# A convolution on four 64-by-64 tiles, its input staged in blocks of 64 tokens, and the first groups transposed inside PSUM

## The chip, the cores and the metric

The kernel runs on one core of one Trainium2 chip. The metric is device time in microseconds (us) of one execution; the kernel before takes 362.98 us (median of three runs, 361.67 to 363.38). The kernels here are told apart by the ratio of mean times of runs made on the same chip in the same rounds, and by their profiles. "Group" below means eight output tiles of 128 tokens; the program has 33 groups.

## The reference, cut to what matters

```python
# attention part: a causal convolution over time, 7 taps, one set of taps per head
w = softmax(weight)                          # 8 heads x 7 taps
y[b, s, h*24+g] = sum_k w[h, k] * x[b, s-6+k, h*24+g]     # B=8, S=4224, D=192
# mixer part
h = (y^T @ U) @ V                            # rank 32, over the whole sequence
u = y + h^T
out = u + relu(u @ w_ch1) @ w_ch2            # 192 -> 768 -> 192
```

The product `y^T @ U` runs over the whole sequence. So no token of a batch can go through the mixer before the convolution of that whole batch is done. The batches then follow one another.

## The kernel before

The convolution is a matmul with a band matrix as the stationary operand. Batch 0 uses the whole 128x128 array; batches 1 to 7 use sixteen 32x32 tiles, so their input lies in blocks of 32 tokens, a quarter of the sequence in each 32 partitions.

```python
def load_x(b, r, ...):                       # GpSimd's queue: fp32 in DRAM, bf16 in SBUF
    n = 4 * n_of(r, NX)
    nc.gpsimd.dma_start(out=x_bufs[b % 2][32 * r : 32 * r + 32, 1 : 1 + n, :], in_=tokens(b, r, 0, n))
    ...                                      # and the six tokens before the quarter

def conv_unit(b, heads):                     # two heads: 64 matmuls
    ps = [bank() for _ in range(4)]
    for i, h in enumerate(heads):
        for k in range(2):                   # this block, the block before
            for r in range(4):               # rows of the array, one PSUM bank each
                for c in range(4):           # columns of the array
                    nc.tensor.matmul(out=..., lhsT=band_of(r, h, k), rhs=x_bufs[b % 2][rows, ...], ...)
    ...                                      # four evictions by ScalarE

# the head of the program: batch 0
for i, (a, e) in enumerate(CHUNKS):          # four chunks of fp32 input, SyncE's queue
    ...cast by ScalarE and VectorE, conv_first(a, e), U's transposes, keep_warm(3), tt_part
tt_split(0, ...); tt_sum(0, "act")
h_unit(0)
transpose_pe(0)                              # u of group 0 by TensorE through PSUM
h_unit(1)
transpose(1)                                 # u of group 1 by a DMA transpose
```

Each group `g` then runs, on TensorE: perhaps a conv unit of a later batch, W1 (36 matmuls), h of group `g+2` (8 matmuls), W2 of group `g-1` (48 matmuls). VectorE adds `u` to what W2 leaves in PSUM, into one of four output tiles, and SyncE's queue stores it. The same queue carries the DMA transposes of `u`.

## Time and profile before

| reading | us |
|---|---|
| median | 362.98 |
| first W1 starts | 35.5 |
| steady group without / with a conv unit | 8.33 / 9.06 |
| one conv unit | 0.72 |
| longest wait of TensorE | 8.1 |

From the page of the kernel before, the slices of the span: the busy share of TensorE in tenths and the clock granted to it. One digit is a fortieth of the span, 9 us.

```profile
PE   5697999994699999999999999999999999999995
PEclk9587899999599999999999999999999999999999
```

The last three quarters of the span are full. What can be won lies in the first eleven slices, about 100 us: the head, and the hole in slices 10 and 11. The table of stretches says the same in numbers. Its columns are the stretch and its length, then for each engine the busy time (and instructions), then the clock, the DMA share and GB/s.

```profile
core 0: us, PE busy (x) PEld busy (x) DVE busy (x) ACT busy (x) POOL busy (x), PEclk, DMA share, GB/s
0.00:35.50 35.50, 25.08 (x191) 14.35 (x194) 14.86 (x46) 13.07 (x26) 10.67 (x23) 0.76 1.05 187
35.50:84.70 49.20, 47.25 (x895) 30.99 (x894) 37.55 (x70) 29.18 (x61) 9.64 (x20) 0.97 1.22 161
84.70:101.30 16.60, 8.51 (x166) 3.72 (x164) 4.30 (x7) 5.65 (x12) 2.51 (x5) 0.69 0.72 118
101.30:362.60 261.30, 255.66 (x4000) 179.14 (x3998) 207.00 (x385) 131.54 (x260) 20.88 (x42) 1.00 0.73 152
```

The hole, in the timeline of TensorE (start, length, engine, line, operation, what it writes and reads, and in brackets the idle time before it and what ended that):

```profile
85.28 0.50 PE L260 MATMUL bank<-x_sb_86,band 32*32 32x216 bf16 x12
93.87 0.39 PE L260 MATMUL bank<-x_sb_86,band 32*32 32x192 bf16 x16 [8.09 <-DMA x_sb_86<-in_x_dram]
...
94.72 6.70 PE L380 MATMUL bank<-uT,W_sb 64*128 64x512 bf16 x36
```

TensorE starts batch 3's convolution (line 260) and waits 8.09 us for its input. The W1 behind it (line 380) takes 6.70 us where 4.06 is usual, because the clock is at half (0.5 from 89.9 to 100.1 us in the clock record). The steady half, from the chain of waits (start, length, what):

```profile
278.31 0.73 PE bank L260 x55
279.04 3.99 PE bank L380 x36
283.03 0.32 PE bank L331 x8
283.35 4.07 PE bank L401 x48
```

Conv unit, W1, h, W2, and nothing but TensorE between them.

### The profile page before, as it was taken

What the parts mean: (1) busy time and instruction counts of PE and PEld (TensorE: products, weight loads), DVE (VectorE), ACT (ScalarE), POOL (GpSimd) and SP (SyncE); (2) the same over time, 40 slices, a digit from 0 to 9 for tenths busy, and PEclk for the clock granted to TensorE, in tenths of its full rate; (3) what the DMA queues carried; (4) which work ended last, traced back from release to release, by engine and by line L of the source; (5) the groups of instructions that cost most, each with busy time, mean ns of one, the idle gap of its engine ahead of it and who ended that gap; (6) DMA issues with size and microseconds to landing.
All of it is one profiled execution on the core that took longest, in us unless ns stands there. A gap on an engine that the chain in (4) does not pass through costs nothing. (4 is left out here: it accounts for less than half of the span.)

```text
span 362.6 us, 12101 instructions
## 1 busy us (share of the span) xinstructions
PE 336.5 (93%) x5248; PEld 228.2 (63%) x5250; DVE 263.7 (73%) x506; ACT 179.4 (49%) x358; POOL 43.7 (12%) x90
## 2 busy tenths in 40 slices
PE   5697999994699999999999999999999999999995
PEld 2363466654277666666666666667666766667775
DVE  4335767863268887888788878887888888888763
ACT  2344774571345546555655554554455355555440
POOL 2143140131101111111111111110000000000000
PEclk9587899999599999999999999999999999999999
DMA  5989999999557997999999988898444556555525
GB/s 161 253 152 181 104 139 217 157 186 200 60 130 114 148 195 142 175 176 177 181 164 180 181 163 164 169 181 170 118 121 129 106 127 174 152 132 132 132 96 167
DMA packets 122837, 56.23 MB, mean 155 GB/s; under 512 B 84224, under 2 KB 122624, under 8 KB 122624
## 3 DMA queue, kind: packets, MB, share of 16 engines
q1 hardware_dynamic: 90512, 42.60, 49.4%
q0 software_dynamic: 32128, 12.83, 32.3%
q8 instruction: 41, 0.67, 0.7%
q14 instruction: 12, 0.10, 0.1%
q10 hardware_dynamic: 144, 0.03, 0.0%
HBM read 28.93 MB, written 25.95 MB: 151 GB/s over the span
## 5 line engine op out<-in xcount | busy, mean ns | idle before, releaser
L380 PE MATMUL bank<-uT,W_sb 64*128 64x512 bf16 x1188 | 139.0, 385 | 0.1
L65 ACT ACTIVATE y_sb<-bank 128x432 bf16<-128x432 f32 (+5 forms) x122 | 51.0, 505 | 105.6 <-PE bank L260 82.1
L380 PEld LDWEIGHTS <-W_sb 64*128 64x128 bf16 x1188 | 57.7, 96 | 69.6 <-issue 10.8
L411 DVE TENSOR_TENSOR o<-bank,u_ring 128x384 f32<-128x384 f32 x132 | 70.6, 553 | 27.8 <-PE bank L401 24.4
L342 DVE TENSOR_TENSOR u_ring<-y_sb,bank 128x384 bf16<-128x384 bf16 (+1 forms) x136 | 64.3, 535 | 3.7 <-PE bank L331 3.6
L260 PEld LDWEIGHTS <-band 32*32 32x32 bf16 x1568 | 15.5, 88 | 18.1 <-DMA x_sb_86<-in_x_dram 8.3
L99 POOL CAST seen<-y_sb 1x1 f32<-1x1 bf16 x24 | 4.2, 173 | 167.4 <-ACT y_sb L65 167.4
L260 PE MATMUL bank<-x_sb_86,band 32*32 32x192 bf16 (+1 forms) x896 | 14.0, 255 | 9.3 <-DMA x_sb_86<-in_x_dram 8.1
L103 POOL DMA_DIRECT2D x_sb_86<-in_x_dram x16 | 12.9, 806 | 5.0 <-PE bank L380 3.1
L331 PE MATMUL bank<-tt_sb,V_sb 32*128 32x192 bf16 x264 | 13.1, 252 | 0.4 <-ACT tt_sb L65 0.4
L331 PEld LDWEIGHTS <-V_sb 32*128 32x128 bf16 x264 | 5.2, 93 | 12.7 <-issue 12.3
L284 PE MATMUL bank<-x_sb_85,band 128*128 128x288 bf16 (+3 forms) x32 | 8.6, 316 | 4.1 <-ACT x_sb_85 L65 3.9
L310 DVE TENSOR_TENSOR lo<-bank,hi 128x192 bf16<-128x192 f32 x8 | 2.9, 358 | 12.9 <-ACT hi L65 12.9
L67 DVE CAST y_sb<-bank 128x288 bf16<-128x288 f32 (+3 forms) x10 | 4.9, 488 | 8.5 <-PE bank L284 8.4
L260 PE MATMUL bank<-x_sb_85,band 32*32 32x192 bf16 (+1 forms) x672 | 9.5, 251 | 1.4 <-issue 0.8
L103 POOL DMA_DIRECT2D x_sb_85<-in_x_dram x12 | 9.7, 807 | 4.4 <-PE bank L380 2.4
L201 PE MATMUL bank<-warm 128*128 128x512 bf16 x23 | 8.6, 508 | 1.3 <-DVE warm L136 1.2
L391 DVE TENSOR_SCALAR rl_1832<-bank 128x512 bf16<-128x512 f32 x2 | 1.4, 692 | 10.9 <-PE bank L380 10.9
L260 PE MATMUL bank<-x_sb_86,bandp 32*32 32x192 bf16 x128 | 8.6, 250 | 0.0
L284 PE MATMUL bank<-x_sb_85,bandp 128*128 128x288 bf16 (+3 forms) x32 | 8.5, 314 | 0.0
L297 PE MATMUL bank<-y_sb,U_sb 128*32 128x192 bf16 x264 | 7.9, 248 | 0.6 <-DVE y_sb L67 0.5
L284 PEld LDWEIGHTS <-band 128*128 128x128 bf16 x32 | 3.7, 120 | 5.7 <-issue 4.5
(323 smaller groups left out, 631.6 us busy)
## 6 DMA issues: line engine op xcount, KB each, us to landing
out_dram<-o SPq DMA_DIRECT2D x132, 192.0 KB, 3.1
x_sb_86<-in_x_dram POOLq DMA_DIRECT2D x12, 384.0 KB, 6.9
x_sb_85<-in_x_dram POOLq DMA_DIRECT2D x9, 384.0 KB, 7.6
x_sb_86<-in_x_dram POOLq DMA_DIRECT2D x4, 432.0 KB, 7.6
x_sb_85<-in_x_dram POOLq DMA_DIRECT2D x3, 432.0 KB, 5.7
xf<-in_x_dram SPq DMA_DIRECT2D x1, 1152.0 KB, 12.7
xf<-in_x_dram SPq DMA_DIRECT2D x1, 960.0 KB, 15.0
W_sb<-in_moe_w_ch_dram POOLq DMA_DIRECT2D x3, 288.0 KB, 6.9
```

The lines of the kernel that those rows point to most:

```text
L65: nc.scalar.activation(out=out_ap, in_=in_ap, func=ACT.Copy)
L67: nc.vector.tensor_copy(out=out_ap, in_=in_ap)
L99: nc.gpsimd.tensor_copy(out=seen[0:1], in_=y_tiles[b - 1][0:1, 0, seen_col : seen_col + 1])
L103: nc.gpsimd.dma_start(out=x_bufs[b % 2][32 * r : 32 * r + 32, 1 : 1 + n, :], in_=tokens(b, r, 0, n))
L201: nc.tensor.matmul(out=ps[:], lhsT=warm[:, 0:P], rhs=warm[:], start=True, stop=True)
L260: nc.tensor.matmul(out=o.rearrange("p (t g) -> p t g", g=nh * GS)[:, :, i * GS : (i + 1) * GS], lhsT=band_of(r, h, k), rhs=x_bufs[b % 2][r ...
L284: nc.tensor.matmul(out=ps[:, :, (h - i) * GS : (h - i + 1) * GS], lhsT=(bandp if k else band)[:, h, :], rhs=x_bufs[0][:, a + 1 - k : e + 1 ...
L297: nc.tensor.matmul(out=ps[q * R : (q + 1) * R, 0:D], lhsT=U_sb[:, j, :], rhs=y_tiles[b][:, j, :], start=before + n < 4, stop=before + n >= ...
L331: nc.tensor.matmul(out=ps[r][:, k * D : (k + 1) * D], lhsT=V_sb[rows, j * P : (j + 1) * P], rhs=tt_tiles[b][rows, :], start=True, stop=True,)
L342: nc.vector.tensor_tensor(out=u_of(t0 + 2 * r + k, n), in0=in3(y_tiles[b][:, j : j + n, :]), in1=in3(ps[r][:, k * D : (k + n) * D].rearran ...
L380: nc.tensor.matmul(out=h1[a][:], lhsT=W1_sb[rows, c, ms], rhs=uT[rows, :, c, :], start=c == 0, stop=c == 2,)
L411: nc.vector.tensor_tensor(out=in3(o[:]), in0=in3(ch[g]), in1=u_of(t0, 2), op=ALU.add)
```

## The change

It means to shorten the first 100 us. Its main parts (smaller ones, such as the order of the softmax's steps, are left out):

1. Conv units of batches 1 to 7 use four 64x64 tiles (16 matmuls instead of 64 for two heads); the input lies in blocks of 64 tokens, half of the sequence in each 64 partitions.
2. Batch 0 has the DMA queues to itself: all else waits for its chunks. More warming matmuls, and five chunks instead of four.
3. Groups 0 and 1 need no `u` of their own. TensorE transposes y into PSUM, adds h to it there, and h also goes into W2's PSUM, so that the output addition takes y.
4. Batches 1 and 2 are loaded as fp32 by SyncE's queue into the buffer that batch 0 used, and cast by ScalarE and VectorE. Batch 3 on is loaded as bf16 by GpSimd's queue as before. The schedule of the conv units is moved back a little.

The core of the diff (cuts marked):

```diff
-        nc.gpsimd.dma_start(out=x_bufs[b % 2][32 * r : 32 * r + 32, 1 : 1 + n, :], in_=tokens(b, r, 0, n))
+    PARTS = [(0, 9), (9, 18), (18, 27), (27, NSL)]
+    def load_part(eng, to, b, part):
+        for r in range(2):
+            ...
+            eng.dma_start(out=to[r * C2 : (r + 1) * C2, q0:q1, :], in_=slots(b, r, q0, q1))   # C2 = 64
+    def load_x(b, part):
+        load_part(nc.gpsimd, x_bufs[b % 2], b, part)
+    def load_f32(b, part):
+        load_part(nc.sync, xf, b, part)
...
+    gate(xf[0:1, CHUNKS[0][0], 0:1])
+    nc.gpsimd.dma_start(out=V_sb[0:R, 0:VA], in_=moe_V[:, 0:VA])
+    nc.gpsimd.dma_start(out=U_in[:], ...)
+    gate(xf[0:1, CHUNKS[2][0], 0:1])
+    ...                                     # W1, the rest of V; W2 behind the last chunk
...
             for k in range(2):
-                for r in range(4):
+                for r in range(2):
...
-                    for c in range(4):
+                    for c in range(2):
                         nc.tensor.matmul(...)
...
+    def add_h(g, ps, parts, engs):          # h into the transposed y, six matmuls
+    def h_in_ch(g):                         # h into W2's PSUM, eight matmuls
...
-    tt_sum(0, "act")
-    h_unit(0)
-    transpose_pe(0)
-    h_unit(1)
-    transpose(1)
+    for part in range(4):
+        load_f32(1, part)
+    ...
+    add_h(0, uT_ps[0], hi0, ("act", "dve", "act"))
+    tt_sum(0, "dve")
+    add_h(1, uT_ps[1], hi0, ("dve", "act", "dve"))
...
-    pre = {1: [(1, 0), (1, 1)], 3: [(2, 0)], 4: [(2, 1), (2, 2)], 5: [(2, 3)]}
-    mid = {1: [(1, 2), (1, 3)]}
+    pre = {2: [(1, 0), (1, 1)], 5: [(2, 0), (2, 1)], 6: [(3, 0)], 7: [(3, 1)], 8: [(3, 2), (3, 3)]}
+    mid = {2: [(1, 2), (1, 3)], 5: [(2, 2), (2, 3)]}
+    casts = {1: [(1, 0, "act"), (1, 1, "act"), (1, 2, "dve"), (1, 3, "act")]}
+    casts.update({3: [(2, 0, "act"), (2, 1, "act")], 4: [(2, 2, "act"), (2, 3, "act")]})
...
+        if g == 3:
+            gate(x_bufs[0][0:1, PARTS[1][0], 0:1])
+            for part in range(4):
+                load_x(3, part)             # all four quarters of batch 3
...
+        if 0 < g < 3:
+            load_f32(2, 2 * g - 2)
+            load_f32(2, 2 * g - 1)
```

## The prediction

> **What bounds the kernel now.** From 101 us on, TensorE: the table of stretches shows it busy nearly throughout at granted clock 1.00, and the chain of waits is matmuls alone: per group 3.99 us for W1, 4.07 for W2, 0.28 for h, and 0.72 for one conv unit (two heads of a batch, 64 small matmuls). Before 101 us it is not. In the timeline the first W1 starts at 35.5 us, though batch 0's last input chunk landed at 20.4; the first landed at 13.4 because all loads shared the queues, and batch 0's conv then ran at clock 0.5. At 85.8 us TensorE waits 8.1 us for batch 3's input (longest in the list of waits), and the W1 after it takes 6.70 us, clock 0.5. [...]
>
> **Conv units.** 64 matmuls of 32x32 tiles become 16 of 64x64. Two 64-row W1 matmuls of 512 columns take 222 ns together, so four of about 396 columns, if the four tiles run side by side, take 172 ns, and a unit 4 x 172 = 0.69 us (estimate). Against 0.72 that is nothing[...]. 28 units: -1 us, within 2.
>
> **Head.** With batch 0 alone, chunk 0 should land near 8.5 us, the last near 16 to 17; more warming matmuls should keep the clock at 1.0. Conv starts near 10.5 us instead of 14.6. The second tt product, its sum, h, addition and transposes leave the chain; h is added to the transposed y in PSUM. After the last landing: cast 0.4, conv 0.5, eviction 0.7, tt 0.3, hi 0.5, h 0.7, eviction 0.7 us. First W1 at 22.5 us (W1's weights, now behind chunk 2, land near 21). Saves 13 us.
>
> **Groups 0 to 7.** From the first W1 to that of group 8: 35.5 to 125.9, 90.4 us. The same work at the durations above is 8 x 8.35 + 12 x 0.73 + 2 x 1.1 = 78 us, so 12.5 us are waits and slow clock: 8.1 + 2.7 around batch 3, 1.6 in the first W1 (5.59 us), the rest batch 1's conv. I expect these gone (batch 3 has some 25 us to arrive), but two new waits: batch 1 through the fp32 buffer, behind V's copies, is cast by 38 us where TensorE is ready at 35.6 (2 us); and batch 4's last two quarters are both requested in group 8, 9 us before they are needed, where two quarters took 11 to 13 us in this trace (2.5 us). Another 1 us for slow clock.
>
> **From group 9** nothing changes: 9.06 us a group with one conv unit.
>
> **Sum.** 363 - 13 - 12.5 + 5.5 - 1 = 342, rounded to 341 us; 8 in 10 between 334 and 350. Faster by over 2%: 0.93; within 2%: 0.06; slower: 0.01.
>
> **Right or wrong.** First W1 at 21 to 25 us; no clock 0.5 between 11 and 22 us; no long wait for batch 3; conv units of 0.65 to 0.8 us; 9.06 us a group in the second half; a wait ahead of batch 1's conv and one ahead of batch 4's.
>
> **What would make it wrong.** Conv tiles that don't overlap (1.4 us a unit, +19 us); the SyncE queue, where batch 1's and 2's loads stand ahead of transposes and outputs; half clock in the head; batch 1 after 40 us.

The sum: 363 - 13 - 12.5 + 5.5 - 1 comes to 342 us, put as 341.

## The result, and the profile after

The new kernel is correct and takes 357.9 us (median of four runs, 357.28 to 358.69), beside 363.18 us of the kernel before in the same rounds. The ratio is 0.9861, with a 95% interval of 0.9822 to 0.9899. Ratios here are the mean time of one kernel's fast runs over that of the other's of the same rounds, so not quite the ratio of the medians. The change is worth 1.4%, inside the 2% band. The prediction was 341 us, with a range of 334 to 350: it missed by 17 us.

The slices of the new kernel:

```profile
PE   8899699966989999999999999999999999999995
PEclk9959989996999999999999999999999999999999
```

The head is fuller, but there are new holes: slice 5, and slices 9 and 10. The start of the first W1 matmul of each group, read from the two traces, says where they lie:

| group | before, start (since the group before) | after, start (since the group before) | after minus before |
|---|---|---|---|
| 0 | 35.52 | 27.59 | -7.9 |
| 1 | 44.03 (8.50) | 31.85 (4.27) | -12.2 |
| 2 | 56.13 (12.10) | 47.81 (15.96) | -8.3 |
| 3 | 65.66 (9.53) | 59.81 (12.00) | -5.9 |
| 4 | 76.34 (10.68) | 68.25 (8.44) | -8.1 |
| 5 | 94.72 (18.38) | 85.77 (17.52) | -9.0 |
| 6 | 107.26 (12.54) | 99.44 (13.67) | -7.8 |
| 8 | 125.91 | 119.87 | -6.0 |
| 32 | 346.56 | 340.67 | -5.9 |

The 12 us won by group 1 are partly given back in group 2. In group 5 the old hole of 18.4 us, which was to close, has become a hole of 17.5 us. From group 8 on, the two kernels run at the same pace.

The longest waits of TensorE in the list of waits (who waited for what: us in total, times, longest):

```profile
PE bank L288 <- DVE o L475: 5.8, 4, 4.0
PE bank L288 <- ACT x_sb_87 L66: 3.4, 1, 3.4
```

Line 288 is the conv unit. The wait for batch 3's input is gone, and these two stand in its place. In the timeline of TensorE:

```profile
40.91 0.66 PE L464 MATMUL bank<-W_sb,rl_487 128*128 128x192 bf16 x6
44.95 0.84 PE L288 MATMUL bank<-x_sb_87,band 64*64 64x408 bf16 x5 [3.38 <-ACT x_sb_87 L66]
...
77.12 0.34 PE L288 MATMUL bank<-x_sb_86,band 64*64 64x408 bf16 x2
81.44 0.36 PE L288 MATMUL bank<-x_sb_86,band 64*64 64x408 bf16 x2 [3.98 <-DVE o L475]
82.52 0.55 PE L288 MATMUL bank<-x_sb_86,band 64*64 64x384 bf16 x4 [0.72 <-DVE o L475]
```

At 41.6 us TensorE is ready for batch 1's convolution and waits for ScalarE's last cast of its input. At 77.5 us it is in the middle of batch 2's and waits for PSUM: VectorE has not drained W2's banks (line 475, the output additions). Each time the clock falls to half behind the wait (44.7 to 48.1 us and 82.2 to 89.1 us in the clock record).

**The first wait is a matter of load rate.** Batch 1's last piece landed at 43.71 us. The stretches of the new kernel while batch 0's first chunk (128 partitions) and batch 1 (64 partitions a transfer) were loaded:

```profile
4.00:7.00 3.00, 3.00 (x8) 1.06 (x7) 1.80 (x9) 0.46 (x2) 0.00 (x0) 1.00 1.07 348
28.00:40.00 12.00, 11.74 (x125) 6.45 (x122) 10.47 (x19) 10.90 (x17) 0.00 (x0) 1.00 1.11 204
```

The last number is GB/s. Both move rows of 768 bytes from DRAM into fp32 buffers by SyncE's queue, and next to nothing else moves meanwhile. The second goes at 204 GB/s instead of 348. At 204 GB/s a batch of 3.24 MB takes 15.9 us; at 330, within the 325 to 348 of batch 0's chunks, it would take 9.8 (both worked out). One difference between the two is the number of partitions that a transfer writes. The experiments test whether it sets the rate.

**The second wait is a matter of what shares the DMA engines.** VectorE's timeline, and the queues of SyncE (SPq) and GpSimd at that time:

```profile
72.61 1.95 DVE L369 TENSOR_TENSOR u_ring<-y_sb,bank 128x384 bf16<-128x384 bf16 x4 [0.19 <-PE bank L358]
80.83 0.56 DVE L475 TENSOR_TENSOR o<-bank,u_ring 128x384 f32<-128x384 f32 x1 [6.26 <-DMA out_dram<-o]
```

```profile
63.68 2.69 SPq L99 DMA_DIRECT2D xf<-in_x_dram  x4
66.48 6.09 SPq L379 DMA_TRANSPOSE uT<-u_ring  x1
72.67 2.68 SPq L476 DMA_DIRECT2D out_dram<-o  x4
75.44 6.80 SPq L379 DMA_TRANSPOSE uT<-u_ring  x1
```

```profile
68.99 5.71 POOL L99 DMA_DIRECT2D x_sb_87<-in_x_dram  x8 [0.28 <-issue]
```

SyncE issues batch 2's second half (63.68), then needs 6.09 us to issue one transpose behind it, then four stores. From 69 us GpSimd asks for all of batch 3. The four stores' data had been ready in SBUF one after another from 66.8 to 68.9 us, so SyncE's queue held them back for about 6 us. The stores issued at 72.67 to 74.91 landed at 80.70 to 84.25, some 8 to 9 us later, where the median is 2.6. All four output tiles are then full, so VectorE waits 6.26 us, W2's PSUM is not drained, and TensorE finds no bank for the convolution.

The steady half, from the chain of waits of the new kernel:

```profile
148.82 0.81 PE bank L288 x13
149.62 3.99 PE bank L426 x36
153.94 4.07 PE bank L464 x48
```

The conv unit takes 0.81 us instead of 0.73. Sixteen matmuls are not quicker than sixty-four.

### The profile page after: what moved, and what is told of

Read it like the earlier page. It is cut to its first block, busy times and chain, and to the rows that moved or that the text cites. A ratio compares the mean times of both kernels' runs of the same rounds, so it can differ in the third digit from the quotient of the medians.

```text
span 356.3 us, 9559 instructions
## 1 busy us (share of the span) xinstructions
PE 338.3 (95%) x3968; PEld 224.4 (63%) x3968; DVE 269.3 (76%) x515; ACT 187.0 (52%) x353; POOL 38.0 (11%) x74
## 4 chain that ended last, share of the span: by engine, by line
PE 77%; DMA 11%; DVE 6%; ACT 2%; POOL 1%; SPq 1%; issue 1%; DVEq 0%; POOLq 0%
PE bank L464 34%; PE bank L426 31%; PE bank L288 6%; DMA xf<-in_x_dram 5%; DMA out_dram<-o 3%; PE bank L324 2%; DMA U_in<-in_moe_U_dram 2%; PE bank L358 2%; DMA x_sb_86<-in_x_dram 2%; PE bank L406 1%; DVE rl_3677 L437 1%; DVE rl_2949 L437 1%; DVE rl_4403 L437 1%; DVE rl_2220 L437 1%; SPq L99 1%; PE bank L311 1%
## 5 line engine op out<-in xcount | busy, mean ns | idle before, releaser
L426 PEld LDWEIGHTS <-W_sb 64*128 64x128 bf16 x1188 | 56.2, 95 | 73.1 <-issue 12.5
L475 DVE TENSOR_TENSOR o<-bank,u_ring 128x384 f32<-128x384 f32 x124 | 66.5, 556 | 31.5 <-PE bank L464 20.8
L66 ACT ACTIVATE y_sb<-bank 128x384 bf16<-128x384 f32 (+3 forms) x103 | 44.3, 510 | 85.6 <-PE bank L288 76.4
L369 DVE TENSOR_TENSOR u_ring<-y_sb,bank 128x384 bf16<-128x384 bf16 (+1 forms) x128 | 60.5, 537 | 2.8 <-PE bank L358 2.7
L288 PEld LDWEIGHTS <-band 64*64 64x64 bf16 x336 | 12.0, 110 | 17.7 <-issue 15.1
L288 PE MATMUL bank<-x_sb_87,band 64*64 64x408 bf16 (+1 forms) x192 | 14.9, 362 | 3.4 <-ACT x_sb_87 L66 3.4
L288 PE MATMUL bank<-x_sb_86,band 64*64 64x408 bf16 (+1 forms) x144 | 12.0, 350 | 6.1 <-DVE o L475 5.8
L99 POOL DMA_DIRECT2D x_sb_87<-in_x_dram x24 | 17.1, 728 | 2.7 <-issue 2.3
L68 DVE CAST y_sb<-bank 128x384 bf16<-128x384 f32 (+2 forms) x24 | 12.5, 564 | 4.6 <-PE bank L288 2.1
L66 ACT ACTIVATE x_sb_86<-xf 128x768 bf16<-128x768 f32 (+8 forms) x11 | 9.7, 913 | 5.4 <-DMA xf<-in_x_dram 5.3
L358 PEld LDWEIGHTS <-V_sb 32*128 32x128 bf16 x248 | 4.5, 92 | 12.5 <-issue 12.4
L99 POOL DMA_DIRECT2D x_sb_86<-in_x_dram x16 | 11.4, 719 | 2.8 <-issue 2.1
L288 PE MATMUL bank<-x_sb_87,bandp 64*64 64x384 bf16 x64 | 11.3, 348 | 0.0
L288 PE MATMUL bank<-x_sb_86,bandp 64*64 64x384 bf16 x48 | 8.4, 339 | 0.0
L324 PEld LDWEIGHTS <-U_sb 128*32 128x32 bf16 x264 | 6.0, 101 | 2.3 <-issue 2.1
```

What stands on the lines that cost most here:

```text
L66: nc.scalar.activation(out=out_ap, in_=in_ap, func=ACT.Copy)
L68: nc.vector.tensor_copy(out=out_ap, in_=in_ap)
L99: eng.dma_start(out=to[r * C2 : (r + 1) * C2, q0:q1, :], in_=slots(b, r, q0, q1))
L288: nc.tensor.matmul(out=ps[r][c * C2 : (c + 1) * C2, :], lhsT=(bandp if r and k else band)[rows, h, to], rhs=x_bufs[b % 2][rows, c + 1 - k ...
L324: nc.tensor.matmul(out=ps[q * R : (q + 1) * R, 0:D], lhsT=U_sb[:, j, :], rhs=y_tiles[b][:, j, :], start=before + n < 4, stop=before + n >= ...
L358: nc.tensor.matmul(out=ps[r][:, k * D : (k + 1) * D], lhsT=V_sb[rows, j * P : (j + 1) * P], rhs=tt_tiles[b][rows, :], start=True, stop=True,)
```

## The experiments

Twelve kernels ran. In each job the kernel before ran alongside; its median was 362.3 to 365.3 us, so ratios compare better than medians across jobs. Each of the twelve ran four times, but e7 once, in an unknown state. All other runs were fast but for one of e4's four, and one of the kernel before's seven in the job of e5 to e7; the ratios leave these two out, the medians do not.

| run | result | median us | ratio to before |
|---|---|---|---|
| new kernel | correct | 357.90 | 0.9861 |
| e1_u_first | correct | 359.65 | 0.9905 |
| e2_warm_u | correct | 359.17 | 0.9885 |
| e3_two_queues | correct | 351.91 | 0.9693 |
| e4_outs8 | correct | 357.39 | 0.9812 |
| e5_full_part | wrong | 348.09 | 0.9586 |
| e6_direct_bf16 | correct | 353.81 | 0.9766 |
| e7_no_b3 (one run, state unknown) | wrong on purpose | 351.63 | |
| e8_full_no_b3 | wrong | 341.94 | 0.9374 |
| e9_spread | correct | 346.24 | 0.9497 |
| e10_spread2 | correct | 342.03 | 0.9373 |
| e11_tiles_only | correct | 361.64 | 0.9905 |
| e12_spread2_warm | correct | 345.94 | 0.9497 |

### e1 and e2: the slow clock in the head

```diff
 e1:
-    nc.gpsimd.dma_start(out=V_sb[0:R, 0:VA], in_=moe_V[:, 0:VA])
     nc.gpsimd.dma_start(out=U_in[:], ...)
+    nc.gpsimd.dma_start(out=V_sb[0:R, 0:VA], in_=moe_V[:, 0:VA])
 e2:
+    keep_warm(6)
     for r0 in range(0, R, 16):              # U's transposes
```

> Change of the new kernel: U is requested before the first part of V, both still behind chunk 0. In the new kernel's timeline U landed at 16.35 us, TensorE stood 1.2 us before the 32 small matmuls that transpose U, and the clock was 0.5 from 17.4 to 27.6 us. Theory A (the late U makes the idle gap and so the slow clock): U lands near 14.5 us, no gap before its transposes, clock 1.0 for most of 17 to 27 us, first W1 at 23.5 to 25 us instead of 27.6, total 2.5 to 4 us less. Theory B (the 32 light matmuls of 32 by 32 themselves count as idle for the clock): the gap goes, the clock still falls to 0.5 after them, first W1 at 26 to 27 us, total about 1 us less.

> Change of the new kernel: six more warming matmuls of 512 columns just before U's transposes, where TensorE waited 1.2 us. Theory A (the gap lowers the clock): clock 1.0 until the first W1, which starts near 24.5 to 25.5 us, total 2 to 3 us less. Theory B (the light matmuls lower it): clock 0.5 all the same from about 17 to 21 us on, first W1 unchanged within 0.5 us or up to 1 us later.

Neither helped: ratios 0.9905 and 0.9885, not better than the new kernel's. In both the first W1 started earlier, at 25.73 and 25.88 us, and the clock was at 0.5 for 3.4 us only. But runs e3, e4, e5, e7 and e8, whose head is the new kernel's or nearly so, also started it at 24.9 to 25.3 us, with a slow spell of 3.4 us. So the profiled run of the new kernel, at 27.6 us, had a longer slow spell: it lasted 10.2 us. The slow spells in the head last 3.4, 6.8 or 10.2 us in the clock records at hand (10.24, 3.41 and 6.83 us in the kernel before, 10.24 in the new kernel), and begin elsewhere in each run (at 17.4 us in the new kernel, 19.4 in e1, 18.9 in e2). Neither edit is shown to do anything, and both theories' sizes are lost in that scatter. Nor did e1 do what it was made for: U landed at 16.09 us instead of 16.35, not at 14.5, and TensorE still waited 0.8 us for it. In e2 the wait for U was gone (0.6 us for VectorE remained) and the clock still fell.

The pair shows another thing. In e1 and e2 group 2's W1 started at 47.96 and 48.84 us, in the new kernel at 47.81, in e4 at 48.04: an earlier head bought nothing, because batch 1 landed near 44 us in all of them.

### e3: half of the staged loads on another queue

```diff
-        for r in range(2):
+        for r, eng in enumerate(engs):      # fp32 loads: (nc.sync, nc.gpsimd)
```

> Change of the new kernel: of the fp32 loads of batches 1 and 2 the half for partitions 64 to 127 is issued from GpSimd's queue, that for 0 to 63 stays on SyncE's; bytes, descriptors and places are the same. In the new kernel these loads moved 203 GB/s (28 to 42 us) where batch 0's 128-partition chunks moved 304 to 334. [...]both halves together move 280 to 340 GB/s, batch 1 has landed by 36 to 38 us instead of 43.7, the 3.4 us wait ahead of its conv and the slow clock after it go, batch 2 lands earlier too and the 4 us and smaller waits on the output additions in group 5 shrink; total 6 to 13 us less. Rival (the rate is set by the strided source or by the descriptors, 768 bytes each): about 200 GB/s in sum, batch 1 lands at 40 us or later, total within 3 us.

The first forecast is that of the theory that the number of partitions that a load writes sets its rate.

It gained 6 us (ratio 0.9693), and the stall of group 5 fell: 11.19 us from W1 to W1 instead of 17.52. For batch 1 it did not do what it was made for. GpSimd's half started at 18 us and took the engines by itself at about 190 GB/s; V's copies came late behind it (TensorE waited 4.1 us for them), and SyncE's half followed at about 188 GB/s, landing at 43.08 us. The halves hardly overlapped, so whether the width of a load sets its rate was not decided. One rival did lose ground: GpSimd's half moved in packets of 4608 bytes and SyncE's in packets of 768, at about the same rate, so the size of the packets does not set it. (The trace gives 325 to 348 GB/s for batch 0's chunks, where the expectation says 304 to 334.)

### e4: eight output tiles

```diff
-    outs = ctx.enter_context(tc.tile_pool(name="outs", bufs=4))
+    outs = ctx.enter_context(tc.tile_pool(name="outs", bufs=8))
```

> Change of the new kernel: eight output tiles instead of four. In the new kernel, in group 5, VectorE waited 6.3 us for an output tile whose store had not landed, and TensorE then waited 5.8 us in all for PSUM that VectorE had not drained, with clock 0.5 behind it. Theory (four output tiles are what passes a late store on to TensorE): the waits on the output additions at 77 to 86 us are gone, group 5 takes about 10 to 11 us instead of 17.5 from first W1 matmul to first W1 matmul, total 6 to 8 us less. Rival (the transposes and loads behind the same queue come late too, so the wait only moves to the next W1 or conv): less than 3 us.

The waits on the output additions are gone and group 5 takes 11.95 us, as the theory says. But group 6 then takes 17.40 us instead of 13.67, and the total is 0.5 us less, or 1.4 us without the slow run (median of three 356.49), as the rival says. From the list of waits of this run, below the 6.1 us for batch 1's cast:

```profile
PE bank L288 <- DMA x_sb<-in_x_dram: 3.6, 3, 2.2
PE bank L426 <- DMA uT<-u_ring: 2.1, 1, 2.1
```

The wait has moved to batch 3's input and to a transpose. The four output tiles only chose who waited; the DMA was late for all.

### e5: full-width loads

```diff
+    nc.gpsimd.memset(xf[:, NT:NSL, :], 0.0)
+
     def load_f32(b, part):
-        load_part(nc.sync, xf, b, part)     # two transfers of 64 partitions
+        q0, q1 = PARTS[part]
+        q1 = min(q1, NT)
+        nc.sync.dma_start(out=xf[:, q0:q1, :],            # one of 128; wrong tokens, on purpose
+            in_=x[b, q0 * P : q1 * P, :].rearrange("(j p) d -> p j d", p=P))
```

> Wrong result on purpose. Change of the new kernel: the fp32 loads of batches 1 and 2 write all 128 partitions in each transfer (batch 0's layout of 128-token blocks, so the conv of these two batches reads wrong tokens); same queue, same 768-byte rows, 3 per cent fewer bytes, four transfers instead of eight. In the two-queue run the GpSimd half alone, in larger packets, also moved only 162 to 189 GB/s into 64 partitions, but the halves hardly overlapped for batch 1[...]. [...]290 to 335 GB/s, batch 1 lands at 34 to 37 us instead of 43.7, no wait over 1 us ahead of its conv, W1 of group 2 starts near 40 us instead of 47.8, and the waits on output additions in group 5 (5.8 us) fall below 2 us; total 9 to 15 us less than the new kernel's 357.9. Rival (strided source, row size or SyncE's queue sets the rate): about 200 GB/s, landing after 41 us, total within 3 us.

Batch 1 landed at 37.32 us instead of 43.71, group 2's W1 started at 41.03 instead of 47.81, and TensorE waited 0.5 us for the cast instead of 3.4. The run took 348.09 us, ratio 0.9586, about 10 us less than the new kernel. The stretch while batch 1 was loaded:

```profile
28.00:34.00 6.00, 6.00 (x65) 2.52 (x60) 5.81 (x11) 5.54 (x10) 0.00 (x0) 1.00 1.10 329
```

That is 329 GB/s instead of 204, with rows of the same size on the same queue. So a load into all partitions brings the rate back. Why it does, the trace does not show. The order of reading DRAM and the number and size of the transfers changed with the width, and e6 speaks to the first. One step missed its number: the waits on output additions fell to 3.5 us and not below 2.

### e6: no staging

```diff
+    for part in range(4):
+        load_x(1, part)                     # GpSimd, bf16, behind W2
...
-    for part in range(4):
-        load_f32(1, part)
...
+        if g == 0:
+            for part in range(4):
+                load_x(2, part)
```

> Change of the new kernel: the fp32 staging of batches 1 and 2 is undone: GpSimd's queue loads them as bf16 straight into the conv's buffers (as the new kernel does for batch 3 on, and the kernel before for all), batch 1 from 18 us on, batch 2 behind it; the casts on ScalarE and VectorE disappear; head, tiles and groups 0 and 1 stay. Theory (what eats the gain is the staging: half-rate loads, and SyncE's queue filled ahead of transposes and outputs): batch 1 lands by 33 us, batch 2 by 45 us, no wait over 1 us in groups 1 to 6, first W1 of group 6 near 82 us instead of 99.4; total 338 to 346 us. Rival (bandwidth as such is short in the first 100 us, whatever the path): waits of 4 us or more move to outputs or transposes, total 350 us or more.

353.81 us: the rival was nearer. Batch 1 landed at 35.46 us; its casts were gone. The stretch from 30 to 35 us shows what a load into 64 partitions with a cast to bf16 does:

```profile
30.00:35.00 5.00, 4.48 (x31) 1.67 (x33) 3.69 (x7) 1.68 (x3) 2.91 (x4) 0.66 1.59 190
```

It writes 190 GB/s, almost the rate of the staged loads, in rows of half the bytes (384 instead of 768), and so it brings twice the tokens, with the same strided reads as the staged loads. So the order of reading does not hold a half-width load at 204 GB/s: here about 380 GB/s were read (twice the 190, worked out from the cast). The rate of the written bytes is about the same in both. But batch 2 followed at once and ran into the transposes:

```profile
PE bank L428 <- DMA uT<-u_ring: 6.0, 2, 4.4
```

The transpose issued at 32.87 us landed at 45.05, 12 us later, where the median is 3.7. (In the new kernel, one issued at 75.44 us took 14.9.)

### e7: batch 3 not loaded

```diff
             gate(x_bufs[0][0:1, PARTS[1][0], 0:1])
-            for part in range(4):
-                load_x(3, part)
```

> Wrong result on purpose. Change of the new kernel: batch 3 is not loaded (its conv reads batch 1's old input). Collision theory (batch 3's eight loads, issued from 69 us, delay the outputs): the waits on output additions in group 5 fall from 5.8 us to under 1.5 us, group 5 takes 10 to 12 us instead of 17.5. Rival (the outputs are late because batch 2's half-rate loads and the transpose stand ahead of them in SyncE's queue, before batch 3's data move at all): 4 us or more of these waits stay.

```profile
PE bank L288 <- ACT x_sb L66: 6.3, 1, 6.3
...
PE bank L288 <- DVE o L475: 1.0, 2, 0.8
```

The waits on output additions fell from 5.8 to 1.0 us, and group 5 took 12.01 us instead of 17.52. The stores were issued as late as before (72.88 to 74.69 us), since SyncE's queue was as full, but landed 4.7 to 5.0 us later instead of 8.0 to 9.3. VectorE still waited 3.1 us for an output tile instead of 6.3. So what makes the stores late is both: SyncE's queue holds them back, and batch 3's eight loads then nearly double the time to landing; without the second TensorE loses 1.0 us. (In e3 batch 3 was loaded, and batch 2's data landed 2.6 us earlier, by 71.64 us instead of 74.28; the hole was gone there too. That fits a collision of the two.) The batch 1 wait stayed and was 6.3 us here, since the head was earlier in this run. The run took 351.63 us; it is a single one.

### e8: both at once

The edits of e5 and e7 together.

> Wrong result on purpose: both e5 and e7 at once (full 128-partition loads of batches 1 and 2, batch 3 not loaded). Theory (the gap between 341 predicted and 357.9 measured is these two things, half-rate staging and the collision of batch 3's loads with outputs and transposes, plus a head that ends near 25 us instead of 22.5): no wait over 1.2 us on TensorE after the first W1, groups 2 and 5 at 11 to 12 us each, first W1 of group 6 at 86 to 88 us, total 342 to 345 us. If something else holds it, 346 or more.

341.94 us, ratio 0.9374. Groups 2 and 5 took 11.71 and 9.83 us, the latter even less than expected; no wait of TensorE after the first W1 was over 1 us; group 6 started at 83.65 us. With the half-width loads and the collision out of the way, the time is within 1 us of the 341 us of the prediction. This kernel does not load batch 3 at all, so it is a bound and not a version; e10 below is the correct one. By medians, e5 gained 9.8 us, e7 6.3, and both together 16.0, so the two about add up (e7 is a single run of unknown state, and the jobs differ).

### e9 and e10: a correct version

e9 takes e6 and lets batch 2's and batch 3's quarters go two per group. A tiny GpSimd copy of one element of a relu's result holds each back:

```diff
+    LOADS = {2: [(0, 2, 0), (5, 2, 1)], 3: [(0, 2, 2), (5, 2, 3)],
+             4: [(0, 3, 0), (5, 3, 1)], 5: [(0, 3, 2), (5, 3, 3)]}
...
+        for m, b, part in LOADS.get(g, []):
+            gate(rl_tiles[g][0][0:1, m, 0:1])
+            load_x(b, part)
```

> Correct. Change of e6 (bf16 loads straight into the conv's buffers, no staging): batch 2's and 3's quarters are let go two per group, in groups 2 to 5, each held back until a certain relu of that group is done, instead of four at once in groups 0 and 3. In e6 the transposes for groups 2, 4 and 5 landed 7 to 12 us after their issue because they shared the DMA engines with these loads, and TensorE waited 6.0 us for them. Theory (bunched loads delay the transposes): those waits fall under 2 us in all, total 343 to 348 us (353.8 in e6). Rival (the bytes of groups 2 to 5 are too many, however spread): waits of 4 us or more for outputs, transposes or batch 3's input remain, total 350 or more.

> Correct. e9 with four more changes: the rest of V is requested ahead of W1, eight output tiles, batch 3's conv units in groups 7 and 8 only (two each), and their evictions shared by ScalarE and VectorE. Expected: the 1.7 us wait for V's copies ahead of h of group 2 goes, small waits on outputs go, W1 of group 8 loses the 0.4 us that it is long in all runs (ScalarE's eight evictions): 2 to 4 us less than e9. If the bytes are the limit (e9's rival), no more than 1 us less.

e10's further edits:

```diff
+    nc.gpsimd.dma_start(out=V_sb[0:R, VA:], in_=moe_V[:, VA:])     # ahead of W1
     nc.gpsimd.dma_start(out=W1_sb[0:C2], in_=w1v)
     nc.gpsimd.dma_start(out=W1_sb[C2:P], in_=w1v)
-    nc.gpsimd.dma_start(out=V_sb[0:R, VA:], in_=moe_V[:, VA:])
...
-    outs = ctx.enter_context(tc.tile_pool(name="outs", bufs=4))
+    outs = ctx.enter_context(tc.tile_pool(name="outs", bufs=8))
...
-    pre = {2: [(1, 0), (1, 1)], 5: [(2, 0), (2, 1)], 6: [(3, 0)], 7: [(3, 1)], 8: [(3, 2), (3, 3)]}
+    pre = {2: [(1, 0), (1, 1)], 5: [(2, 0), (2, 1)], 7: [(3, 0), (3, 1)], 8: [(3, 2), (3, 3)]}
...
-            conv_unit(b, [2 * u, 2 * u + 1], ("act", "dve", "act", "dve") if b < 3 else ("act",) * 4)
+            conv_unit(b, [2 * u, 2 * u + 1], ("act", "dve", "act", "dve") if b < 4 else ("act",) * 4)
```

e9 took 346.24 us and its waits for transposes are gone (the one for group 2 landed 4.0 us after its issue). Waits of 1.5 us on an output addition and 1.1 us on input remained. e10 took 342.03 us, ratio 0.9373 (0.9309 to 0.9437): 6.3% faster than the kernel before, and about 5% faster than the change as it was made. e10's gain over e9 was 4.2 us, at the upper end; its four edits were not tested apart. Its clock in the head was slow for 10.2 us in the profiled run and its first W1 started as late as 27.49 us, so in that run all it gained came after the head:

```profile
27.50:84.70 57.20, 56.84 (x720) 36.48 (x718) 50.13 (x95) 30.92 (x59) 12.75 (x24) 1.00 1.08 170
```

TensorE is busy for 56.84 of 57.20 us at full clock, in the part where the new kernel had both its holes. The bytes of this part were not too many; they only had to be spread.

### e11: the tiles alone

The kernel before with only its conv units and their loads changed to 64x64 tiles and 64-token blocks (GpSimd's queue, bf16).

> Correct. The kernel before with one part of the change alone: conv units of batches 1 to 7 on four 64 by 64 tiles, input in 64-token blocks loaded by GpSimd's queue as bf16; head, schedule and group 0 as before. In the new kernel a conv unit in the second half takes 0.81 us where the kernel before takes 0.72. Theory (the tiles by themselves save nothing): 0.79 to 0.83 us a unit, 9.14 instead of 9.06 us a group with one unit, and the 8 us wait for batch 3 near 86 us stays; total within 4 us of the kernel before. Rival (fewer, larger matmuls save time on TensorE or in the loads): 5 us or more less.

361.64 us, ratio 0.9905 (0.9852 to 0.9959): about 1% less, and within the 4 us. A conv unit took 0.81 us and a group with one 9.14 us; group 5 still took 18.21 us, with 6.4 us of wait for input at one time. The tiles by themselves gain nothing on TensorE; where the 1% comes from was not traced.

### e12: filler among the light matmuls

```diff
+    keep_warm(5)
+    wps = bank()
     for r0 in range(0, R, 16):
         for r in range(16):
             nc.tensor.matmul(out=ups[:, r, :], lhsT=U_in[...], rhs=ident[0:NU, 0:NU], ...)
+            if r % 4 == 3:
+                nc.tensor.matmul(out=wps[:], lhsT=warm[:, 0:P], rhs=warm[:], start=True, stop=True)
```

> Correct. e10 with heavy filler in the head: five warming matmuls of 512 columns before U's 32 light transposing matmuls and one after each four of them. In all runs but e6 the clock fell to 0.5 in the window that holds U's transposes, for 3.4 or 10.2 us[...]; filling only the gap before them (e2) did not stop it. Theory (light matmuls count as idle for the clock): no clock of 0.5 between 8 and 30 us, first W1 at 23.5 to 25.5 us (27.5 in e10), total 0 to 3 us less than e10. Rival[...]: 0.5 appears all the same and the filler costs 1 to 2 us.

345.94 us: 4 us more than e10. U's transposes stretched from 2.1 to 5.2 us, the first W1 started at 29.13 us, and the clock fell all the same. So the rival was nearer, though it said 1 to 2 us. In the profiled run 1.6 us of the loss lies ahead of the first W1; another 2.0 us is a wait for batch 4's input ahead of group 9's W1, which e10 does not have, and which is not explained. The stretches of this run say something about the clock:

```profile
18.13:21.54 3.41, 3.41 (x27) 2.11 (x26) 0.00 (x0) 0.85 (x2) 3.41 (x7) 1.00 1.09 219
21.54:24.96 3.42, 3.42 (x46) 2.64 (x48) 1.42 (x3) 0.49 (x1) 2.09 (x3) 0.50 1.43 199
```

TensorE had no gap from 18.13 to 21.54 us, with 21 of U's light matmuls (32 rows, 32 columns) and six of 128x512, and the clock went to half at the end of it. Its last wait (0.9 us) had ended at 17.11 us, so here the clock fell without a gap in the 4.4 us before. The theory that light matmuls count as idle fits this, but does not explain e6: there the same 32 light matmuls followed a wait of 1.3 us, and the clock stayed at 1.0 from 6.6 to 30.5 us. The runs do not show what lowers the clock here.

## Why the prediction was wrong, point by point

- **"Batch 1 ... is cast by 38 us where TensorE is ready at 35.6 (2 us)."** This step failed. The prediction names no rate, but 38 us is about what batch 0's rate gives: V's copies landed by 26.7 us, and 9.8 us at 330 GB/s (325 to 348 measured) and a cast follow. A transfer into 64 partitions moved 204 GB/s and batch 1 landed at 43.7 us. TensorE was ready at 41.6 us and waited 3.4 us in the profiled run; where the head was earlier, it waited 5.4 to 6.3 us (e1, e2, e4, e7). Either way group 2's W1 started near 48 us, and what the head had won above that was lost. e5, with full-width loads, landed batch 1 at 37.3 us and brought about 10 us back. The prediction had listed "batch 1 after 40 us" among what would make it wrong.
- **"I expect these gone (batch 3 has some 25 us to arrive)."** The wait for batch 3 went, but this step put nothing in its place at group 5. Batch 3's eight loads, the tail of batch 2's and the transposes met in one stretch; stores took 8 to 9 us, and group 5 took 17.5 us. e7 shows that it takes batch 3's loads, on top of SyncE's full queue; e4 that four output tiles only choose the victim. The prediction named SyncE's queue as a danger, rightly, without a number in the sum.
- **"First W1 at 22.5 us", "Saves 13 us."** It was 27.6 us in the profiled run and 24.9 to 25.3 us in five runs with the same head or nearly so. The sum followed the last chunk alone. But TensorE still had work queued: it was busy for 7.48 of the 7.60 us from 16.4 to 24.0 us, with U's transposes (2.1 us, held back by U's landing at 16.35 us), chunk 3's convolution, the tt products and the transposes of group 1. **"More warming matmuls should keep the clock at 1.0"** failed too: 0.5 from 17.4 to 27.6 us. The landings were right: chunk 0 at 7.4 us (8.5 said; 13.4 in the kernel before), the last at 17.0. So was the shorter chain behind the last chunk; what was off is its size and the clock.
- **"A unit 4 x 172 = 0.69 us."** It measured 0.81 us, 0.12 us more than the estimate. The starts of the matmuls in the trace say where: in the twelve units from 139 us on that it holds whole, the first three rounds of four matmuls start 0.17 us apart in the mean, as estimated, but from the last round's start to W1's first matmul 0.29 us pass instead of 0.17. So the rounds run at the estimated rate, and what the estimate left out is the step to W1; the old unit has that step too (0.31 us). The conclusion, that this part is worth nothing, held: group pace 9.14 instead of 9.06 us with one unit, and the offset between the kernels stayed at 5.9 to 6.3 us from group 8 to the end. The dangerous case, tiles that don't overlap (1.4 us), did not happen. 16 matmuls of 384 or 408 columns took 0.81 us, where one after the other they would take four times 0.69 us by the estimate.
- **"Batch 4's last two quarters ... (2.5 us)."** They were requested in group 8 and TensorE waited 0.24 us. This term was too big.
- **The sum.** The sum puts 78 us of work and 5.5 us of waits between the first W1 and group 8's. In the profiled run it was 92.3 us. With the half-width loads and batch 3's removed it was 78.8 us and the run 341.9 us (e8); in e10, which loads everything, it was 78.4 us. So the durations of the work were counted rightly; the two DMA terms were missing or too small, and they are the 16 us between e8 and the new kernel. That e8 comes so near to 341 is partly luck: its head ended 2.8 us later than said, and its waits were nearly 5 us fewer than the sum allowed.

## What to carry to other kernels

Read the rate of a load from a transfer of the same shape: a load into half of the partitions ran at 204 GB/s where a full-width one ran at 329 to 348. If a matmul layout asks for half-width inputs, loading them as bf16 brings about twice the tokens in the same time (190 GB/s written, half the bytes a token). When a buffer more removes a wait and the total stays (e4: 357.4 us instead of 357.9), the resource behind it is late for everyone: spread its load in time (e9 against e6: the same batches two quarters per group instead of four at once, 346.2 us instead of 353.8). And time won in a prologue counts only up to the next arrival that does not depend on it.
